# Token mixer of an attention and mixer kernel: the second token product of three batches by seven block products, added into XT by accumulating DMA

## The chip, the cores and the metric

The kernel runs on one core of a Trainium2 chip. The metric is the device time in microseconds (us); lower is better. A core has four engines that compute: TensorE (PE in the profile; its weight loads are PEld), VectorE (DVE), ScalarE (ACT) and GpSimd (POOL). A fifth, SyncE (SP), issues DMA transfers; ScalarE and GpSimd can issue them too. All transfers run on the same 16 DMA engines. SBUF is the on-chip memory with 128 partitions, PSUM the small memory of eight banks that TensorE writes to, and HBM the memory outside.

## What is computed

Four batches of 768 tokens with eight heads of 64 go through an attention with a hash mask. The result, 512 wide, goes through a mixer: a token part, which mixes the 768 tokens of a batch by way of 256 hidden rows, and a channel part by way of 1536 hidden columns.

```python
x  = attn_out.transpose(0, 2, 1, 3).reshape(B, S, H * D)   # 4 x 768 x 512
xt = x.transpose(0, 2, 1)
h  = np.maximum(xt @ w_tok1, 0.0) @ w_tok2                 # the token part
u  = x + h.transpose(0, 2, 1)
h2 = np.maximum(u @ w_ch1, 0.0) @ w_ch2                    # the channel part
return u + h2
```

All of it is float32; the weights come as 64-bit words and are turned into float32 on the chip. The change lies in the token part, at `@ w_tok2` and at `x + h`.

## The kernel before

The program is one sequence of three stages, and within each stage the order on every engine is the order in which the code is written (with small shifts where the builder interleaves independent work). An engine takes its instructions in that order; one that waits holds up all behind it.

**Attention** (`attention`, the first 317 us) leaves its result in XT, an SBUF tile of 128 partitions x 4 channel blocks x 3072 tokens: the transposed x. `bounce` (line 236) writes each pair of channel blocks to HBM, turned by VectorE 32 x 32 at a time, and `fetch` (line 251) reads a batch back with tokens on the partitions. During this stage the class `Conversion` (line 140) turns the weights W1, W2 and WC1 into float32.

**Tokens** (`tokens`, line 598, from 317 to 400 us) is the stage of the change. For each batch b, `mix1(b)` multiplies x by W1 (line 629: two banks of 128 x 512, six products each), and ScalarE writes the Relu to r1 (line 636). `mix2(b)` multiplies r1 by W2: for each of four channel blocks and two halves of the tokens, two products of 128 x 384 add up in a bank (line 648), and VectorE adds the bank into XT in place (line 654). The order is mix1(0), mix1(1), mix2(0), mix1(2), mix2(1), mix1(3), mix2(2), mix2(3). Between these, `job()` takes the next piece of side work from a list: two sums of the first channel weights (`weight_sums`, line 668, 7 us of VectorE together), and then the conversion of the second channel weights in eight steps (`Conversion.one`, line 220). A step is five VectorE operations on 768 columns (lines 179 to 199), a square on ScalarE that is written over the raw words (line 208), and an ending on VectorE (line 209) which sets very small words to zero. `inputs(0, T, 0)` (line 587) makes two of the operands of the next stage from XT, after mix2(1).

**Channels** (`channels`, line 687, from 400 us) computes the channel part for 1024 tokens at a time, three times. It already uses a scheme of seven products of blocks in place of eight (`hidden`, `product`): sums and differences of blocks are prepared on VectorE, and the seven results are put together by additions. While the first 1024 tokens go through `hidden` (six times, 12 us each), a list made by `prepare` (line 966) is worked off, one entry in the middle of each `hidden` and one after it: sums of the second weights WC2 into SW2, and their blocks stored to HBM by SyncE. In the second `hidden`, `residual(0)` (line 1197) has SyncE write XT of these tokens to the output, to which the results of the channel part are later added by accumulating DMAs that GpSimd issues (line 1154). At its end a flag is tested; a slower path for large inputs follows, which these inputs do not take.

Of the kernel before, what the change touches and what calls it, by code (L numbers as in the profile page):

```python
# [36 lines left out]
F32 = mybir.dt.float32  # L37
# [11 lines left out]
def kernel(  # L49
# [13 lines left out]
    nc = tc.nc  # L63
# [76 lines left out]
    class Conversion:  # L140


        def __init__(self, pool, parts, bufs):
            self.pool, self.bufs = pool, bufs
            self.todo = [
                (w, dst, rows, j, n)
                for w, dst, rows, blocks in parts
                for j in range(*blocks, rows)
                for n in range(0, dst.shape[2], NW // rows)
            ]  # L150
            self.fetched, self.begun, self.ready = [], None, None
            for _ in range(bufs - 1 or 1):
                self.fetch()

        def fetch(self):
# [15 lines left out]
        def begin(self):  # L171
            if not self.fetched:
                return
            raw, to, rows = self.fetched.pop(0)
            hi = raw[:, :, 1]
            tmp = self.pool.tile([P, 2, NW], F32, name="tmp", tag="cvt", bufs=self.bufs - 1)
            big = tmp[:, 0].bitcast(U32)

            nc.vector.tensor_scalar(
                big, hi, 3, 0x3FFFFFFF, op0=ALU.logical_shift_left, op1=ALU.bitwise_and,  # L180
            )
            nc.vector.scalar_tensor_tensor(
                big, hi, 0xC0000000, big, op0=ALU.bitwise_and, op1=ALU.bitwise_or,
            )
            self.begun = raw, tmp, to, rows
# [16 lines left out]
        def end(self):  # L202

            if not self.ready:
                return
            size, big, to, rows = self.ready
            self.ready = None
            nc.scalar.activation(size, size, ACT.Square)
            nc.vector.scalar_tensor_tensor(
                to, size.rearrange("p (t n) -> p t n", t=rows), LEAST * LEAST,  # L210
                big.rearrange("p (t n) -> p t n", t=rows), op0=ALU.is_ge, op1=ALU.mult,
            )
# [4 lines left out]
            self.fetch()  # L217
            self.begin()

        def one(self):  # L220

            before, self.ready = self.ready, None
            self.begin()
            self.join()
            self.ready, after = before, self.ready
            self.end()
            self.ready = after
            self.fetch()

    pairs = [(b, hp) for b in range(B) for hp in range(NP)]  # L230

# [1 line left out]
    dram = ctx.enter_context(tc.tile_pool(name="dram", bufs=1, space=bass.MemoryType.DRAM))  # L233
    bounced = [dram.tile([S, DM], F32, name=f"bounced{b}") for b in range(B)]

    def bounce(pool, n):

        b, hp = pairs[n]
        stage = pool.tile([P, S // 32, 2, 32], F32, name="stage", tag="stage", bufs=1)
        for k in range(2):  # L240
            nc.vector.transpose(
                stage[:, :, k], XT[:, hp + k, S * b : S * b + S].rearrange("p (a i) -> p a i", i=32),
            )
        to = bounced[b].rearrange("(a i) (g c) -> g i a c", i=32, g=4)
        for g in range(4):
            nc.sync.dma_start(
                out=to[g, :, :, 32 * hp : 32 * hp + 64],
                in_=stage[32 * g : 32 * g + 32].rearrange("p a k i -> p a (k i)"),
            )
# [16 lines left out]
    def attention(pool, psum, W1, W2, x0):  # L266
# [202 lines left out]
        for n in range(len(pairs)):  # L469
            halves = [Half(n, half) for half in range(2)]  # L470
            if n:
                load_v(n + 1)
            for now in halves:
                now.scores()
                now.add()
                if now.half == 0:
                    now.add_last()
            if before:
                before.sums()
            if n + 1 < len(pairs):  # L480
                hashes(n + 1)
            halves[1].add_last()
            if n == 0:
                load_v(1)
            load_qk(n + 2)
            add_values(n)
            if before:
                before.newton()
            weights.join()
            halves[0].weigh()  # L490
            if n + 1 == len(pairs):
                before.divide()
                before = Quotients(halves)
                before.sums()
                before.newton()
                weights.turnover()
                halves[1].weigh()
                break
            if before:
                before.divide()  # L500
            weights.turnover()
            halves[1].weigh()
            if n and n % 2 == 0:
                bounce(pool, n - 2)
            if n == 2 * NP:
                fetch(0, x0)
            before = Quotients(halves)
# [87 lines left out]
            nc.vector.tensor_tensor(T[1], XT[:, high, b], T[0], op=ALU.subtract)  # L595
            nc.vector.tensor_tensor(T[3], XT[:, high, a], T[1], op=ALU.subtract)

    def tokens(pool, psum, W1, W2, x0, weights, jobs, T):

        x1 = pool.tile([P, NR, DM], F32, name="x1", tag="x1", bufs=1)
        R1 = {}
        turned = not jobs
        if not turned:
            fetch(1, x1)
            jobs = jobs(weights(pool))
            bounce(pool, len(pairs) - 2)

        def job():
            if not turned and jobs:
                jobs.pop(0)()

        def bank(name):
            return psum.tile([P, 512], F32, name=name, tag="mm", bufs=4 if turned else 8)

        def banks():
            return psum.tile([P, 2, 512], F32, name="trp", tag="tr", bufs=2)

        def mix1(b):
            x = (x0, x1)[b % 2]
            if b and turned:
                turn(b, x, banks)
            r1 = pool.tile([P, NJ, DM], F32, name="r1", tag="r1", bufs=2)
            for j in range(NJ):
                ps = bank("t1")
                for r in range(NR):
                    nc.tensor.matmul(  # L629
                        ps, W1[:, r, P * j : P * j + P], x[:, r], start=(r == 0), stop=(r == NR - 1),  # L630
                    )
                to = r1[:, j]
                if not turned:
                    to = to.rearrange("p (c g i) -> p g c i", c=NCB, i=32)
                    ps = ps.rearrange("p (g c i) -> p g c i", c=NCB, i=32)
                nc.scalar.activation(to, ps, ACT.Relu)
                job()
            R1[b] = r1
            if not turned and b + 2 < B:
                fetch(b + 2, x)  # L640

        def mix2(b):
            r1 = R1.pop(b)
            for cb in range(NCB):
                for half in range(2):
                    ps = bank("t2")
                    for j in range(NJ):
                        nc.tensor.matmul(  # L648
                            ps[:, :HALF], r1[:, j, P * cb : P * cb + P],
                            W2[:, j, HALF * half : HALF * half + HALF],  # L650
                            start=(j == 0), stop=(j == NJ - 1),
                        )
                    u = XT[:, cb, S * b + HALF * half : S * b + HALF * half + HALF]
                    nc.vector.tensor_tensor(u, ps[:, :HALF], u, op=ALU.add)
                if cb % 2:
                    job()

        for b in range(B):
            mix1(b)
            if b:  # L660
                mix2(b - 1)
            if b == 2:
                inputs(0, T, 0)
        mix2(B - 1)
        while not turned and jobs:
            job()

# [19 lines left out]
    def channels(pool, psum, SW1, second, TA, judge):  # L687
# [278 lines left out]
        def prepare():  # L966
# [42 lines left out]
            def hidden_parts(name):  # L1009
# [6 lines left out]

            sums = weight_sums(WC2, SW2, slice(0, HC), slice(HC, NHT), low, high)
            return [
                sums, [whole("p1"), second_parts("p7")], *([second_parts(name)] for name in ("p6", "p3", "p5", "p2", "p4")),
                *([hidden_parts(name)] for name in SMALLER),  # L1020
            ]

# [277 lines left out]
    def attention_and_tokens(W1, W2, x0):  # L1300
# [11 lines left out]
        second["tile"] = second_tile  # L1312

        def weights(pool):
            return Conversion(pool, [(w_ch2, WC2, 3, (0, NHT))], bufs=3)

        def jobs(conversion):
            return [
                *weight_sums(
                    WC1, SW1, slice(0, NCB // 2), slice(NCB // 2, NCB),  # L1320
                    slice(0, DCH // 2), slice(DCH // 2, DCH),
                ),
                *[conversion.one] * (NHT * DM // NW + 1),
            ]

        inside(tokens, W1, W2, x0, weights, jobs, [TA[:, 0], None, TA[:, 1], None])

    def careful_attention_and_tokens(W1, W2, x0):
        def weights(pool, psum):
            conversion = Conversion(pool, [(w_tok1, W1, 3, (0, NR)), (w_tok2, W2, 1, (0, NJ))], bufs=3)  # L1330
            while conversion.fetched or conversion.ready:
                conversion.one()

        def turned(pool, psum):
            turn(0, x0, lambda: psum.tile([P, 2, 512], F32, name="trp", tag="tr", bufs=2))
# [2 lines left out]
        inside(weights)  # L1338
        inside(turned)
        TA = big["TA"]  # L1340
        inside(tokens, W1, W2, x0, None, None, [TA[:, 0], None, TA[:, 1], None])

    with_token_weights(attention_and_tokens)
    flags = []
# [47 lines left out]
```

## Time and profile before

| what | us |
| --- | --- |
| three runs | 808.86, 809.01, 808.11 (median 808.86) |
| profiled execution | 808.87, of which the profile shows a span of 807.1 |
| token stage | 316.89 to 399.57 |
| first token products (L629), busy | 41.8, 96 records |
| second token products (L648), busy | 41.8, 128 records |
| additions into XT (L654) | 32 of 0.552 each |
| an accumulating store to HBM, 512 KB (L1154) | 5.7 to 11.6 from issue to landing, median 7.7 |

A float32 product is two records on TensorE. Records of matmuls overlap, so a product's price is the length of a stretch over the number of products in it, not the mean of a record. In the lists of instructions in order of time, a line has start, length, engine, line of the code, operation, output and input; what stands in brackets is the time for which the engine stood idle before it, and what ended that. The chain that ended last follows the work back from the last instruction; what lies on it sets the end.

### The profile page before, as it was taken

What the parts mean: (1) busy time and instruction counts of PE and PEld (TensorE: products, weight loads), DVE (VectorE), ACT (ScalarE), POOL (GpSimd) and SP (SyncE); (2) the same over time, 40 slices, a digit from 0 to 9 for tenths busy, and PEclk for the clock granted to TensorE, in tenths of its full rate; (3) what the DMA queues carried; (4) which work ended last, traced back from release to release, by engine and by line L of the source; (5) the groups of instructions that cost most, each with busy time, mean ns of one, the idle gap of its engine ahead of it and who ended that gap; (6) DMA issues with size and microseconds to landing.
All of it is one profiled execution on the core that took longest, in us unless ns stands there. A gap on an engine that the chain in (4) does not pass through costs nothing.

```text
span 807.1 us, 10537 instructions
## 1 busy us (share of the span) xinstructions
PE 798.4 (99%) x3901; PEld 475.0 (59%) x3901; DVE 662.0 (82%) x869; ACT 427.7 (53%) x675; POOL 42.6 (5%) x69
## 2 busy tenths in 40 slices
PE   9999999999999999999999999999999999999996
PEld 5544444444444444455544448876666886666885
DVE  4789999999998677899475969888669897778985
ACT  5688888888888886121022221237773335775111
POOL 1000000000000000000010110011100012000001
PEclk9999999999999999999999999999999999999999
DMA  4435353537353424561008994499754578730455
GB/s 161 143 137 159 120 160 121 160 120 238 128 162 107 140 65 159 178 232 59 0 9 301 325 339 178 162 284 257 252 142 138 218 206 203 239 107 1 166 178 106
DMA packets 88490, 132.30 MB, mean 164 GB/s; under 512 B 29480, under 2 KB 62704, under 8 KB 86128
## 3 DMA queue, kind: packets, MB, share of 16 engines
q1 hardware_dynamic: 82320, 112.60, 41.5%
q0 software_dynamic: 5552, 18.35, 9.4%
q8 instruction: 33, 0.54, 0.3%
q10 hardware_dynamic: 560, 0.61, 0.2%
q14 instruction: 25, 0.20, 0.1%
HBM read 97.21 MB, written 33.69 MB: 162 GB/s over the span
## 4 chain that ended last, share of the span: by engine, by line
PE 97%; DVE 1%; SPq 1%; issue 0%; DMA 0%; ACT 0%; DVEq 0%; ACTq 0%
PE b L715 50%; PE sc L345 19%; PE acc L397 15%; PE t L629 5%; PE t L648 5%; PE sums L421 2%; PE hp L306 1%; DVE esd L383 1%; SPq L316 1%; PE hw L324 0%; PE idle L459 0%; DMA bits<-g 0%; DVE esd L379 0%; DVE bits L326 0%; DVE esd L386 0%
## 5 line engine op out<-in xcount | busy, mean ns | idle before, releaser
L352 ACT ACTIVATE e<-sc 128x768 f32<-128x768 f32 x192 | 154.2, 811 | 14.9 <-PE sc L345 14.6
L345 PE MATMUL sc<-qk 64*128 64x384 f32 x768 | 157.0, 487 | 0.0
L715 PE MATMUL b<-R,second 128*128 128x256 f32 (+1 forms) x612 | 150.9, 404 | 0.0
L721 ACT COPY c<-b 128x512 f32<-128x512 f32 (+1 forms) x78 | 37.5, 488 | 187.4 <-PE b L715 174.0
L715 PEld LDWEIGHTS b<-R,second 128*128 128x128 f32 x612 | 116.3, 190 | 31.6 <-issue 17.0
L397 PE MATMUL acc<-e,vn 128*64 128x384 f32 x768 | 127.6, 488 | 0.0
L383 DVE TENSOR_TENSOR esd<-esd,e 128x768 f32<-128x768 f32 x96 | 92.0, 958 | 10.0
L397 PEld LDWEIGHTS acc<-e,vn 128*64 128x64 f32 x768 | 53.6, 137 | 73.3 <-issue 72.0
L345 PEld LDWEIGHTS sc<-qk 64*128 64x128 f32 x768 | 68.0, 187 | 47.8 <-issue 45.7
L715 PE MATMUL b<-XT,WC 128*128 128x256 f32 (+1 forms) x264 | 82.5, 457 | 0.0
L715 PEld LDWEIGHTS b<-XT,WC 128*128 128x128 f32 x264 | 50.2, 190 | 29.6 <-issue 25.1
L345 PE MATMUL sc<-bits 64*128 64x384 bf16 x384 | 64.1, 323 | 0.8 <-DMA bits<-g 0.6
L379 DVE SCALAR_TENSOR_TENSOR esd<-e 128x768 f32<-128x768 f32 x32 | 30.3, 948 | 19.5 <-ACT e L352 19.4
L629 PE MATMUL t<-x,W 128*128 128x512 f32 x96 | 41.8, 593 | 0.0
L648 PE MATMUL t<-W,r 128*128 128x384 f32 x128 | 41.8, 486 | 0.0
L442 ACT COPY rec<-rec 32x384 f32<-32x384 f32 x64 | 32.6, 509 | 10.0 <-DVE rec L436 9.5
L345 PEld LDWEIGHTS <-bits 64*128 64x128 bf16 x384 | 20.2, 94 | 26.8 <-DMA bits<-g 1.4
L648 PEld LDWEIGHTS t<-W,r 128*128 128x128 f32 x128 | 24.3, 190 | 17.6 <-issue 1.4
L715 PE MATMUL b<-XT,SW 128*128 128x256 f32 (+1 forms) x120 | 34.6, 422 | 0.0
L715 PE MATMUL b<-TA,WC 128*128 128x512 f32 x72 | 33.8, 592 | 0.0
L715 PE MATMUL b<-TA,SW 128*128 128x512 f32 x72 | 32.9, 592 | 0.0
L756 POOL TENSOR_TENSOR c<-c 128x512 f32<-128x512 f32 x6 | 8.0, 1339 | 456.7 <-ACT c L721 435.2
(177 smaller groups left out, 1093.2 us busy)
## 6 DMA issues: line engine op xcount, KB each, us to landing
second<-left SPq DMA_DIRECT2D x18, 1344.0 KB
raw<-in_moe_w_ch SPq DMA_DIRECT2D x16, 768.0 KB
qk<-in_qk SPq DMA_DIRECT2D x15, 768.0 KB
seen<-in_qk POOLq DMA_DIRECT2D x21, 384.0 KB, 3.8
WC<-hidden_left SPq DMA_DIRECT2D x15, 448.0 KB
vn<-in_v SPq DMA_DIRECT2D x16, 384.0 KB
vt<-in_vT SPq DMA_DIRECT2D x16, 384.0 KB
bounced<-stage SPq DMA_DIRECT2D x32, 192.0 KB
```

Source lines behind the costliest of these rows:

```text
L306: nc.tensor.matmul(ps[32 * j : 32 * j + 32, :HALF], projblk, loaded[n][0][:, j % 2, sl], start=True, stop=True,)
L345: nc.tensor.matmul(sc[:, i, :HALF], t[rows, 1, P * c : P * c + P], t[rows, 0, qs], start=start, stop=not start,)
L352: nc.scalar.activation(e, sc[:, :, :HALF], ACT.Exp, scale=SCALE)
L379: nc.vector.scalar_tensor_tensor(self.d, es[0], NR * EPS, es[1], op0=ALU.add, op1=ALU.add,)
L383: nc.vector.tensor_tensor(self.d, self.d, e, op=ALU.add)
L397: nc.tensor.matmul(acc[D * i : D * i + D], vn[:, i, c], e[:, i], start=(c == 0), stop=(c == NR - 1),)
L421: nc.tensor.matmul(ps[at : at + 32], ones[:, :32], self.halves[h].d[:, i], start=True, stop=True,)
L442: nc.scalar.copy(rec[other : other + 32, h], rec[at : at + 32, h])
L629: nc.tensor.matmul(ps, W1[:, r, P * j : P * j + P], x[:, r], start=(r == 0), stop=(r == NR - 1),)
L648: nc.tensor.matmul(ps[:, :HALF], r1[:, j, P * cb : P * cb + P], W2[:, j, HALF * half : HALF * half + HALF], start=(j == 0), stop=(j == NJ ...
L715: nc.tensor.matmul(ps, left(k), right(k), start=start and k == ks[0], stop=stop and k == ks[-1], skip_group_check=True,)
L721: nc.scalar.copy(c, ps)
```

## The change

For batches 1, 2 and 3, r1 (256 x 512, transposed) and W2 (256 x 768) are each taken as 2 x 2 blocks. Four sums of blocks of r1 (`left_sums`) and four of W2 (`weight_sums`, once) are made by VectorE, and seven products take the place of eight, in two halves m of 128 rows each: seven products of 128 x 384 in four banks, three of them added to what a bank already holds after that has been copied. Batch 0 keeps its eight products a half. In all batches the results no longer go from the bank into XT: ScalarE copies, and for batches 1 to 3 VectorE and GpSimd additions, leave them in one of three places (the later SW2, 1536 columns each, taken in turn), and GpSimd issues a DMA of 768 KB that adds a place into XT.

```diff
-        def mix2(b):
-            r1 = R1.pop(b)
-            for cb in range(NCB):
-                for half in range(2):
-                    ps = bank("t2")
-                    for j in range(NJ):
...
-                    u = XT[:, cb, S * b + HALF * half : S * b + HALF * half + HALF]
-                    nc.vector.tensor_tensor(u, ps[:, :HALF], u, op=ALU.add)
-                if cb % 2:
-                    job()
+        def left_sums(b):
+            r1, new = R1[b]
+            a00, a01, a10, a11 = (r1[:, k, NQ * i : NQ * i + NQ] for i in range(2) for k in range(2))
+            nc.vector.tensor_tensor(new[:, 1], a00, a10, op=ALU.subtract)
+            nc.vector.tensor_tensor(a10, a10, a11, op=ALU.add)
+            nc.vector.tensor_tensor(new[:, 0], a10, a00, op=ALU.subtract)
+            nc.vector.tensor_tensor(new[:, 2], a01, new[:, 0], op=ALU.subtract)
+
+        def mix2(b, m):
...
+            ps = [bank("t2")[:, :HALF] for _ in range(4)]
+            to = places[(2 * b + m + 1) % 3].rearrange("p (i n t) -> p i n t", i=2, n=2)
+            p1, u, p7, p57 = (to[:, i, n] for i in range(2) for n in range(2))
+
+            def store():
+                nc.gpsimd.dma_start(
+                    out=XT[:, m::2, S * b : S * b + S], in_=to.rearrange("p i n t -> p i (n t)"),
+                    accum_op=ALU.add,
+                )
...
+            product(0, a00, b00)
+            nc.scalar.copy(p1, ps[0])
+            product(1, a01, b10)
+            product(2, s1, sums[:, 0])
+            nc.scalar.copy(p57, ps[2])
+            product(3, new[:, 1], b01)
+            nc.scalar.copy(p7, ps[3])
+            product(0, new[:, 0], sums[:, 1], False)
+            nc.scalar.copy(u, ps[0])
+            product(2, new[:, 2], b11, False)
+            product(3, a11, sums[:, 2], False)
+            nc.vector.tensor_tensor(p1, ps[1], p1, op=ALU.add)
+            nc.gpsimd.tensor_tensor(p57, p7, p57, op=ALU.add)
+            nc.vector.tensor_tensor(p57, p57, u, op=ALU.add)
+            nc.vector.tensor_tensor(p7, ps[3], u, op=ALU.add)
+            nc.vector.tensor_tensor(u, ps[2], u, op=ALU.add)
+            store()
 
         for b in range(B):
             mix1(b)
             if b:
-                mix2(b - 1)
-            if b == 2:
-                inputs(0, T, 0)
-        mix2(B - 1)
+                left_sums(b)
+                mix2(b - 1, 0)
+                job()
+                mix2(b - 1, 1)
+            if b == 1:
+                weight_sums()
+        mix2(B - 1, 0)
+        inputs(0, T, 0)
+        mix2(B - 1, 1)
```

The conversion of the second channel weights is changed with it. The square goes to a tile of its own (`apart`, one buffer) and no longer over the raw words; the joined words have one buffer instead of two in this stage; and a step (`slot` in place of `one`) first ends the words of the step before, then fetches, begins and joins the next ones.

```diff
-            tmp = self.pool.tile([P, 2, NW], F32, name="tmp", tag="cvt", bufs=self.bufs - 1)
+            tmp = self.pool.tile([P, 2, NW], F32, name="tmp", tag="cvt", bufs=1)
...
-            nc.scalar.activation(size, size, ACT.Square)
+            hi = size
+            if self.apart:
+                size = self.pool.tile([P, NW], F32, name="size", tag="size", bufs=1)
+            nc.scalar.activation(size, hi, ACT.Square)
...
-        def one(self):
-
-            before, self.ready = self.ready, None
+        def slot(self):
+
+            self.end()
+            self.fetch()
             self.begin()
             self.join()
-            self.ready, after = before, self.ready
-            self.end()
-            self.ready = after
-            self.fetch()
```

Smaller parts: the last `bounce` uses the third place as its staging tile; the two sums of the first channel weights are one job; the list of `prepare` begins with an empty entry, so that its first sums, which write over the places, come after the first `hidden` and all later entries half a `hidden` later; `inputs(0, T, 0)` stands between the two halves of batch 3. In the order in which SyncE issues its transfers, the builder now has the four writes of `residual(0)` and the store of p1's weights inside the token stage: the first write waits for the DMAs into XT of batch 0, the other three and the store stand behind those of batch 1.

## The prediction

> **What bounds the kernel now.** I read the busy shares first, then the chain that ended last, as shares and then in order of time through the token stage. Busy times alone would not do: a matmul's recorded length overlaps the next one's.
>
> ```profile
> PE 798.4 (99%) x3901; PEld 475.0 (59%) x3901; DVE 662.0 (82%) x869; ACT 427.7 (53%) x675; POOL 42.6 (5%) x69
> PE 97%; DVE 1%; SPq 1%; issue 0%; DMA 0%; ACT 0%; DVEq 0%; ACTq 0%
> ```
>
> TensorE is busy for 99% of the span and carries 97% of the chain. The chain in order of time (start, length, what):
>
> ```profile
> 316.89 20.80 PE t L629 x48
> 337.69 10.32 PE t L648 x32
> 348.01 10.30 PE t L629 x24
> 358.31 10.32 PE t L648 x32
> 368.63 10.30 PE t L629 x24
> 378.93 20.64 PE t L648 x64
> 399.57 364.23 PE b L715 x1308
> ```
>
> Each piece begins where the last one ends: no gap from 316.89 to 763.8. So a matmul less is time less, and a wait of TensorE is time lost. One second product of a batch (L648) takes 10.32 us for 16 products of 384 columns (each is two records): 20.64/32 = 0.645 us a product. A first product (L629) takes 10.30 us.
>
> The same stretches in the table of busy times by stage (PE, PEld, DVE, ACT, POOL, then clock, DMA share, GB/s):
>
> ```profile
> 316.89:378.93 62.04, 62.04 (x162) 30.60 (x162) 54.99 (x71) 13.27 (x19) 0.00 (x0) 1.00 0.49 165
> 378.93:399.57 20.64, 20.64 (x66) 12.16 (x65) 11.14 (x18) 0.60 (x1) 0.00 (x0) 1.00 0.00 1
> ```
>
> VectorE is nearly as full as TensorE up to 379 us (54.99 of 62.04), then half empty; ScalarE is mostly free, GpSimd idle, and the DMA engines rest after 379 us.
>
> **What the Trainium skill says.** (1) *SBUF — State Buffer*, "Who interferes with whom": a VectorE instruction with two SBUF inputs and a GpSimd instruction that reads SBUF exclude each other for a whole instruction. The trace agrees. On VectorE and GpSimd:
>
> ```profile
> 419.64 1.28 POOL L756 TENSOR_TENSOR c<-c 128x512 f32<-128x512 f32 x1 [10.75 <-ACT c L721]
> 419.71 1.63 DVE L993 TENSOR_TENSOR seen<-second 128x384 f32<-128x384 f32 x1
> ```
>
> The L993 that meets the GpSimd addition takes 1.63 us; the next one, at 426.36, takes 0.55. (2) *DMA: Bandwidth & Descriptors*, "Queues, rings and completion order": each DMA engine goes round-robin between the queues with work. Accumulating stores (L1154) agree roughly: landing took 5.7 us at 788.44, where nothing else ran, and 11.6 us at 539.34, beside a 1,344 KB load.
>
> **The change part by part, against the span of 807.1 us.**
>
> *Matmuls, on the path.* Batches 1 to 3: 14 products instead of 16, as large as before. 3 x 2 x 0.645 = **-3.87 us**. Batch 0 keeps its 16.
>
> *Copies, on ScalarE, hidden.* 8 for batch 0 and 24 for the others, about 0.49 us each (L721): 16 us in 80 us in which it was busy for 14. Inside a block of seven, a bank's second product waits for the copy of its first: three products (1.94 us) lie between for p1, two (1.29 us) for the others, so a prompt copy costs nothing.
>
> *VectorE, off the path while not late.* It loses 32 additions of 0.55 (L654), and gains 24 additions, 12 left sums of 256 columns (0.42, as L1123) and 4 sums of W2 (0.56, as L994): together about +3 us. The first left and W2 sums end near 353 us and are needed at 359.6.
>
> *Weight words.* The squares go to their own tile (one buffer), so a raw buffer is free a little later or sooner, never on the path: loads that were waited for nowhere keep 5 us or more. The joined words have one buffer instead of two, and a slot ends the previous words before it begins new ones. VectorE now waits for the square, which stands behind a Relu and so behind TensorE; and a square waits for VectorE's previous ending, with copies that TensorE needs queued behind it. The closest case is the last square (378.2 us), which needs the ending at 378.2 worked out below: 0.5 us before it hurts. I take 0, with 1 us as the other bound; a gain is excluded, since TensorE never waited here. In the attention stage the buffer count was already one: nothing changes.
>
> *Last transposes into a place, first two sums as one job, inputs moved.* The transposes still start the stage; the sums run back to back as before. T[0] is ready near 397.8 and is needed 3.44 us into the hidden products: nothing.
>
> *Sums of the second weights half a step later.* They end near 417 instead of 416.4, as TensorE arrives sooner; the steps after them follow within 4 us of before, and SyncE's stores with them. Four operations (2.1 us) move ahead of the first output products on VectorE; the operand built there at 475.26 is used near 485. Hidden.
>
> *Residual writes.* SyncE's queue has three of the four, and the 768 KB store of p1's weights, behind the landing of batch 1's second accumulating store. They leave the crowded 424 to 436 us, where they held nobody up, and meet the next accumulating store, below.
>
> *Accumulating DMAs: the new wait.* Eight of 768 KB, from three places. Block (3,1) (batch 3, second half) fills the place that block (2,0) still sends. ScalarE's p1 copy waits for that landing; behind it queue the other copies of the block, and TensorE's fifth product waits for p1. When does it land?
>
> - VectorE. The step that ends slot 5's words starts when its square is done, 358.35 + 0.49 + 0.91 = 359.75 (Relu L636 and square L208). Then a slot (0.93 + 4.05 = 5.0), left sums 1.7, additions of (1,0) 2.0, slot 5.0, additions of (1,1) 2.0, slot 5.0, last ending 0.93, left sums 1.7, additions of (2,0) 2.0: 385.0. GpSimd's three additions in this stretch, 1.27 x 384/512 = 0.95 each, hold VectorE up by 0 to 2.9: I take 2.9, as VectorE has no gap here. So (1,1) is done at 377.3 and (2,0) at 387.9.
> - Transfer. GpSimd takes 1.21 us to issue (L1154), data begin 0.35 later, landing is noticed 0.4 after the last data (estimated from the store at 788.44, whose data ran from 790 to 793.7: 3.64 us of all engines for 512 KB). For 768 KB inside SBUF there is no row: 2.35 us at the rate of plain traffic (335 GB/s), 5.5 us at the accumulating rate. I take the middle, 4.0.
> - (1,1) lands at 377.3 + 1.21 + 0.35 + 4.0 + 0.4 = 383.3. Then 3 x 512 + 768 KB of SyncE's writes run from 384.3 for 6.5 us (2.36 MB at 0.36 MB/us, rows at 428 to 436), to 390.8. (2,0)'s data begin at 389.5, share 1.4 us with them, and land at 389.5 + 4.0 + 1.4 + 0.4 = 395.3.
> - Need. Block (3,1) begins at 391.4 (399.57 - 3.87 - 4.5, and 0.2 for a bank that VectorE frees late); its fifth product is due 2.58 later, 393.9, so the landing is due at 393.3, 0.63 earlier for copy and handovers. It is late by 2.0, with the 0.2: **+2.2 us**.
>
> Sum: -3.87 + 2.2 = **-1.7 us**, a span of 805.4. The profiled execution took 808.87, the median of the three is 808.86: **807.2 us**. Each us on the transfer counts twice, as batch 1's store also releases SyncE's writes: between 2.35 and 5.5 the sum runs from -3.7 to +1.3.
>
> **The rivals.**
>
> - *No new wait.* Transfers of under 3 us, or VectorE not held up by GpSimd: both put the landing before 393.3 and leave the whole 3.87 us: 805.0 us. For it: plain traffic runs at 335 GB/s. Against: L1154 moved 144.
> - *The wait eats the gain.* At 4.9 us a transfer the landing is near 397.1: 808.9 us. For it: 5.5 is what the only accumulating row scales to.
> - *Slower.* The accumulating DMA inside SBUF is slower than into HBM, as each 3 KB row is read twice and written once there. Place: the same copy. Price: 2 us for each us beyond 4.9; it is 1.6 us slower from 5.7 us on, and at 6.5 gives +3.3: 812.2 us. For it: beside other traffic a store took 11.6 us. A wait beyond 3.4 us might also cost TensorE its clock (*TensorE: Matmul & The Clock Gate*, "What's actually happening"); no gap that long is in this trace.
>
> **How the numbers follow.** Chances: a wait of about 2 us (807.2) 0.40; no wait (805.0) 0.25; gain eaten (808.9) 0.17; slower (812.2) 0.18. 0.2%, or 1.6 us, is about what a measurement of this kernel can tell from no change. Half of the first case lies beyond it: faster 0.46, same 0.36, slower 0.18. Range: 804.7, the full gain and 0.3 for the spread of the runs, to 810.2, a transfer of 5.5 us; about 0.15 lies above.
>
> **What would show it.** Right: 28 records for each of batches 1 to 3, no gap of TensorE before 391, one gap near 394 whose releaser is ScalarE's p1 copy, itself released by the DMA into XT; the issue of (2,0)'s store near 388; landing times of 6 to 8 us. Wrong: a gap at a block's first products (VectorE late with sums or banks), a gap behind a square, or gaps in the hidden products from the shifted weights; no gap at all says that transfers or VectorE are faster than taken.

## The result and the profile after

The changed kernel takes 817.6 us (median of six runs, 815.75 to 819.71), the kernel before 808.9 in the same series (808.11 to 810.19): a ratio of 1.0107, with a 95% interval of 1.0089 to 1.0125. The forecast was 807.2 us with a range from 804.7 to 810.2, so the kernel became slower where a gain was forecast, and its time lies outside the range. The profiled execution took 816.98 us, with a span of 815.1 where before it was 807.1.

On the page of the profile after, the busy shares and the shares of the chain:

```profile
PE 799.5 (98%) x3889; PEld 473.8 (58%) x3889; DVE 667.7 (82%) x877; ACT 441.5 (54%) x707; POOL 60.1 (7%) x83
PE 92%; DVE 3%; issue 2%; POOL 1%; SPq 1%; ACT 0%; DMA 0%; DVEq 0%; POOLq 0%; ACTq 0%
```

Twelve product records fewer, as meant, and yet TensorE shows more busy time, so some records are longer. Its share of the chain falls from 97% to 92%; VectorE goes from 1% to 3%, and GpSimd and "issue" (an engine that waits for nothing that the profile shows) come in. The chain in order of time (start, length, what):

```profile
317.61 20.80 PE t L639 x48
...
359.03 9.04 PE t L690 x28
...
368.08 0.55 DVE second L705
...
381.78 0.99 POOL second L706
...
389.75 1.21 POOL XT L673
390.96 1.03 POOL second L706
391.99 6.96 issue
...
398.96 1.22 POOL XT L673
400.18 1.04 POOL second L706
...
401.24 0.56 DVE second L707
...
402.78 1.21 DVE TA L592
...
405.04 0.56 DVE second L705
...
405.65 24.71 PE b L774 x53
```

The saving is there: a batch of seven products takes 9.04 us instead of 10.32. But from 368.07 to 405.65 no piece of the chain is TensorE's. To 381.78 it is mostly VectorE's work (left out here but for its first line). Then it hangs on GpSimd: the addition of block (2,0) (L706), the store of that block (L673 at 389.75), the addition of block (2,1) behind it, then 6.96 us in which GpSimd seems to wait for nothing, the next store, the next addition, and only then VectorE, which ends with the addition (L705) that the hidden stage waits for. The stretches around the two stops of TensorE, in the table of busy times (PE, PEld, DVE, ACT, POOL, then clock, DMA share, GB/s):

```profile
394.88:399.26 4.38, 0.00 (x1) 0.00 (x1) 0.00 (x0) 0.53 (x2) 0.30 (x1) 1.00 0.54 100
399.26:403.20 3.94, 3.89 (x6) 1.67 (x6) 1.93 (x4) 1.19 (x3) 1.95 (x2) 0.57 0.69 125
403.20:405.65 2.45, 0.00 (x1) 0.00 (x1) 2.45 (x4) 0.00 (x0) 0.03 (x1) 1.00 0.66 120
405.65:412.00 6.35, 6.35 (x11) 2.79 (x12) 3.70 (x5) 0.58 (x1) 2.21 (x2) 0.73 0.68 124
```

TensorE stands still for 4.38 us, does its last three products at a clock of 0.57 (3.89 us where 3 x 0.645 = 1.94 would do), stands still again for 2.45, and starts the hidden stage at 0.73. Against the span of before:

| where | us |
| --- | --- |
| the token stage starts later (317.61 for 316.89; it lies between 316.4 and 317.8 in all these profiles, changed or not) | +0.72 |
| six products fewer | -3.87 |
| stop before the fifth product of block (3,1) | +4.38 |
| slow clock in the three products after it (3.89 us for 1.94) | +1.95 |
| stop before the hidden stage (2.49 in the list of TensorE's instructions) | +2.49 |
| short waits before 394.88 (what is left of the stage) | +0.4 |
| hidden and later products, 366.2 us instead of 364.23: the slow start | +1.96 |
| sum | +8.0 |

Two waits have to be explained, then, and the clock follows them. ScalarE's list of instructions names the cause of the first one:

```profile
398.73 0.48 ACT L695 COPY second<-t 128x384 f32<-128x384 f32 x1 [7.20 <-DMA XT<-second]
```

The copy of p1 stood for 7.20 us until the store of block (2,0) had landed. This is the wait that the prediction named. For the second one, GpSimd's list:

```profile
389.75 1.21 POOL L673 DMA_DIRECT2D XT<-second  x1 [6.99 <-DVE second L709]
...
398.96 1.22 POOL L673 DMA_DIRECT2D XT<-second  x1 [6.97 <-issue]
...
405.62 1.21 POOL L673 DMA_DIRECT2D XT<-second  x1 [4.41 <-DVE second L705]
```

The store at 398.96 has had its data since 393.64 (the end of VectorE's last addition of that block). It comes 0.3 us after the store of 389.75 has landed (8.9 us from issue to landing, at 398.65); the next one, 405.62, again comes 0.3 us after a landing (6.3 us from 398.96). GpSimd seems unable to have two of these transfers in flight. The store at 389.75, by contrast, waited for its data: VectorE was done with them at 389.34. The releaser in brackets of the last line, L705, is an addition of block (3,1), which this store doesn't need; its own data were ready at 402.86.

The addition of block (3,0) stands on GpSimd behind the store of 398.96 and begins at 399.74. VectorE had waited for it for 7.13 us when it went on at 401.24. Behind that stand the rest of that block's additions, then the two operations of `inputs` (L592, L593), which the change has moved between the halves of batch 3, and only then L705. So both stops go back to the landing at 398.65: the first directly, by the place, the second by way of GpSimd's queue. But `inputs` is part of the second stop too: it takes VectorE from 402.78 to 405.04, 2.26 us, with a stop of 2.49. No run puts it behind L705.

### The profile page after: what moved, and what is told of

It is laid out like the page before. It is cut to its first block, busy times and chain, and to the rows that moved or that the text cites. A ratio compares the mean times of both kernels' runs of the same rounds, so it can differ in the third digit from the quotient of the medians.

```text
span 815.1 us, 10615 instructions
## 1 busy us (share of the span) xinstructions
PE 799.5 (98%) x3889; PEld 473.8 (58%) x3889; DVE 667.7 (82%) x877; ACT 441.5 (54%) x707; POOL 60.1 (7%) x83
## 4 chain that ended last, share of the span: by engine, by line
PE 92%; DVE 3%; issue 2%; POOL 1%; SPq 1%; ACT 0%; DMA 0%; DVEq 0%; POOLq 0%; ACTq 0%
PE b L774 49%; PE sc L345 18%; PE acc L397 15%; PE t L639 4%; PE sums L421 2%; PE t L682 1%; PE t L690 1%; PE hp L306 1%; DVE esd L383 1%; PE hw L324 1%; SPq L316 1%; POOL second L706 0%; PE idle L459 0%; POOL XT L673 0%; DVE tmp L179 0%
## 5 line engine op out<-in xcount | busy, mean ns | idle before, releaser
L774 PE MATMUL b<-R,second 128*128 128x256 f32 (+1 forms) x612 | 150.9, 404 | 0.0
L774 PEld LDWEIGHTS b<-R,second 128*128 128x128 f32 x612 | 116.3, 190 | 31.6 <-issue 17.2
L383 DVE TENSOR_TENSOR esd<-esd,e 128x768 f32<-128x768 f32 x96 | 92.0, 958 | 10.0
L774 PE MATMUL b<-XT,WC 128*128 128x256 f32 (+1 forms) x264 | 84.3, 464 | 2.5 <-DVE second L705 2.5
L774 PEld LDWEIGHTS b<-XT,WC 128*128 128x128 f32 x264 | 50.7, 192 | 34.0 <-issue 26.0
L673 POOL DMA_DIRECT2D XT<-second x8 | 9.9, 1237 | 385.3 <-ACT second L686 340.2
L774 PE MATMUL b<-XT,SW 128*128 128x256 f32 (+1 forms) x120 | 34.6, 422 | 0.0
L774 PE MATMUL b<-TA,WC 128*128 128x512 f32 x72 | 33.8, 592 | 0.0
L774 PE MATMUL b<-TA,SW 128*128 128x512 f32 x72 | 32.9, 592 | 0.0
L386 DVE TENSOR_TENSOR esd<-esd,e 128x768 f32<-128x768 f32 x32 | 30.5, 953 | 1.8
L639 PEld LDWEIGHTS t<-x,W 128*128 128x128 f32 x96 | 18.2, 190 | 22.7 <-issue 21.5
```

The costliest lines, as they stand in the source:

```text
L383: nc.vector.tensor_tensor(self.d, self.d, e, op=ALU.add)
L386: nc.vector.tensor_tensor(self.d, self.d, self.es[-1], op=ALU.add)
L639: nc.tensor.matmul(ps, W1[:, r, P * j : P * j + P], x[:, r], start=(r == 0), stop=(r == NR - 1),)
L673: nc.gpsimd.dma_start(out=XT[:, m::2, S * b : S * b + S], in_=to.rearrange("p i n t -> p i (n t)"), accum_op=ALU.add,)
L774: nc.tensor.matmul(ps, left(k), right(k), start=start and k == ks[0], stop=stop and k == ks[-1], skip_group_check=True,)
```

## The experiments

Two theories stood at the start. **A (queue)**: GpSimd can't issue an accumulating store while another is in flight, and the additions queued behind it come late. **B (place)**: the wait of block (3,1) for its place is the only cause, and the second stop and the clock follow from it. All results in one table; the token stage runs from its first product to the first product of the hidden stage in the chain, "rest" from there to the end of the span, both from the one profiled execution, and the ratio is to the kernel before, timed on the same chip.

| kernel | median us | ratio, 95% interval | token stage | rest |
| --- | --- | --- | --- | --- |
| before | 808.9 | | 82.68 | 407.5 |
| changed | 817.6 | 1.0107 (1.0089 to 1.0125) | 88.04 | 409.5 |
| ring_after | 812.82 | 1.0042 (1.0025 to 1.0058) | 85.48 | 409.0 |
| fourth | 816.57 | 1.0086 (1.0073 to 1.0099) | 87.67 | 409.7 |
| fourth_ring | 814.28 | 1.0051 (1.0037 to 1.0065) | 84.48 | 410.6 |
| ring_before | 809.60 | 0.9999 (0.9989 to 1.0008) | 82.67 | 407.6 |
| dve57 | 811.48 | 1.0032 (1.0020 to 1.0044) | 84.05 | 408.0 |
| fourth_dve57 | 805.21 | 0.9954 (0.9940 to 0.9967) | 78.81 | 408.2 |
| fourth_dve57_ring | 805.99 | 0.9957 (0.9943 to 0.9970) | 78.81 | 407.6 |
| no_residual | 814.11 | 1.0063 (1.0047 to 1.0078) | 85.56 | 410.2 |
| eight | 808.87 | 0.9993 (0.9984 to 1.0001) | 82.67 | 407.7 |

### More room for GpSimd's descriptors (ring_after, ring_before)

```diff
-        "TRN2", target_bir_lowering=False, num_devices=1, dynamic_dma_scratch_size=1024
+        "TRN2", target_bir_lowering=False, num_devices=1, dynamic_dma_scratch_size=1600
...
-    projs = const.tile([P, P + 32], F32, name="projs")
...
     def attention(pool, psum, W1, W2, x0):
+        projs = pool.tile([P, P + 32], F32, name="projs", tag="projs", bufs=1)
```

> The changed kernel with a descriptor area for GpSimd's DMAs of 1,600 instead of 1,024 bytes a partition (to make room, the projections are kept in the attention stage's pool). Theory A (queue): GpSimd can't issue an accumulating store while the one before it is in flight, and the additions queued behind it on GpSimd come late; then VectorE's inputs and the last block, and with them the start of the hidden stage at 405.65, hang on GpSimd. Expected under A: store (2,1) is issued near 394 instead of 398.96, the 2.49 us idle time ahead of the hidden stage goes (it starts near 403.4), the clock is back by then, 813 to 814 us; the 4.4 us idle time ahead of the fifth product stays. Theory B (place): the prediction's wait for the landing of block (2,0) is the only cause, and the rest follows from it: store (2,1) is still issued at 398.9, 817.6 us as before this edit.

> The kernel before with 1,600 instead of 1,024 bytes for GpSimd's descriptors (projections moved as in the others): the control. Theory A: its accumulating stores to HBM (L1154) are issued as soon as VectorE has their data, where the page of before shows 660.60 right behind a landing at 660.27; nobody waits for them, so within 0.2% of 808.9. Theories B and C: the same time, issues unchanged.

Measured: 812.82 us, a ratio of 1.0042, just under the band of theory A. GpSimd's list in ring_after:

```profile
388.67 1.20 POOL L673 DMA_DIRECT2D XT<-second  x1 [6.94 <-DVE second L709]
...
392.97 1.20 POOL L673 DMA_DIRECT2D XT<-second  x1 [2.07 <-DVE second L709]
```

The store of (2,1) now goes out 4.30 us after that of (2,0), which lands only at 397.3: two are in flight, and the 6.97 us of "issue" are gone. The second stop is gone as well; the first remains, at 4.06 us. Theory A holds for the stores, and B, which left no room for this, falls. In the kernel before, the same limit was there and cost nothing. Its GpSimd list, and then that of ring_before:

```profile
539.34 1.21 POOL L1154 DMA_DIRECT2D out<-second  x1 [2.42 <-DVE second L1140]
551.27 1.21 POOL L1154 DMA_DIRECT2D out<-second  x1 [10.72 <-DVE XT L784]
```

```profile
537.65 1.20 POOL L1154 DMA_DIRECT2D out<-second  x1
540.86 1.20 POOL L1154 DMA_DIRECT2D out<-second  x1 [2.01 <-DVE XT L781]
```

Before, 11.9 us lie between these two stores, and the first takes 11.6 to land; with more room it is 3.2 us. The time is the same, since nobody waits for them.

### Another place for block (2,0) (fourth, fourth_ring)

```diff
-            to = places[(2 * b + m + 1) % 3].rearrange("p (i n t) -> p i n t", i=2, n=2)
+            to = x0.rearrange("p r c -> p (r c)")[:, : 2 * S]
+            if turned or (b, m) != (2, 0):
+                to = places[(2 * b + m + 1) % 3]
+            to = to.rearrange("p (i n t) -> p i n t", i=2, n=2)
```

> The changed kernel with block (2,0) sent from a part of x0, free since the first products of batch 2, so that block (3,1) fills a place from which nothing is being sent. Theory A (queue): the idle time of 4.38 us ahead of 399.26 and the slow products behind it go, but the hidden stage still starts near 405.6, since GpSimd's stores and the additions behind them stand where they did: one idle time of 7 to 8 us ahead of the hidden stage, at least as much lost to the clock there as now, 817 to 818.5 us. Theory B (place): the idle time, the slow products and the slow start of the hidden stage go together, 807 to 810 us.

Measured: 816.57 us, a little under the band, and the intervals of this ratio and of the changed kernel's overlap. TensorE's list in fourth (the edit adds three lines, so here and in all kernels that have it L777 is L774, L676 is L673, and so on):

```profile
395.27 0.81 PE L693 MATMUL t<-W2sums,r 128*128 128x384 f32 x2
404.53 5.09 PE L777 MATMUL b<-XT,WC 128*128 128x512 f32 x8 [8.45 <-DVE second L708]
```

The first stop is gone; TensorE is done with the stage at 396, and then stands for 8.45 us, since the hidden stage starts about where it did. The wait that the prediction had named could be removed whole without a gain: behind it, the chain by way of GpSimd was nearly as late. That is A's forecast and speaks against B.

> Both edits together: 1,600 bytes a partition for GpSimd's descriptors, and block (2,0) sent from x0. Theory A (queue): no idle time above 1 us from 388 us to the hidden stage, clock at full there, hidden stage from 397 to 398: 806 to 807.5 us, faster than the kernel before. Theory B (place): the same as with x0 alone. Theory C (the accumulating DMAs themselves, by their traffic or by GpSimd's use of the SBUF port, slow the rest): still above 811 us.

This one missed: 814.28 us instead of 806 to 807.5, in the band of theory C. TensorE still stands 5.34 us before the hidden stage, at 402.27. VectorE's list in fourth_ring:

```profile
396.39 0.56 DVE L710 TENSOR_TENSOR second<-second 128x384 f32<-128x384 f32 x1 [2.22 <-POOL second L709]
...
397.92 1.22 DVE L592 TENSOR_TENSOR TA<-XT 128x1024 f32<-128x1024 f32 x1
399.05 2.70 DVE L593 TENSOR_TENSOR TA<-XT 128x1024 f32<-128x1024 f32 x1
401.68 0.54 DVE L708 TENSOR_TENSOR second<-t,second 128x384 f32<-128x384 f32 x1
```

With free places and free issue, the addition on GpSimd (L709 in this kernel) still stands in GpSimd's queue behind the store of the block before, and that store waits for VectorE's last addition of its block; VectorE in turn waits 2.2 us a block for GpSimd's addition (as at 396.39). The two engines take turns instead of working side by side. L593, which meets the next GpSimd addition at 399.19, takes 2.70 us where L592 takes 1.22. And the addition that the hidden stage waits for (L708) stands behind both, so 3.76 us of VectorE's list ahead of it, from 397.92 to 401.68, are those of `inputs`. So theory A was incomplete: a store that blocks is one part of it, an addition placed behind a store is another, and where `inputs` stands is a third.

### The addition of p7 and p57 on VectorE (dve57, fourth_dve57, fourth_dve57_ring)

```diff
-            nc.gpsimd.tensor_tensor(p57, p7, p57, op=ALU.add)
+            nc.vector.tensor_tensor(p57, p7, p57, op=ALU.add)
```

> The changed kernel with one edit: the addition of p7 to p57 (L706) runs on VectorE instead of GpSimd, so nothing that VectorE waits for stands behind an accumulating store on GpSimd. Theory A (queue of GpSimd): the stores are issued as late as before this edit (store (2,1) only after (2,0) has landed, near 398), so the idle time of about 4.4 us ahead of the fifth product of block (3,1) and the slow products behind it stay; but VectorE reaches the last block's additions early, and the hidden stage follows the last product without the 2.49 us idle time: 812 to 814 us, ratio near 1.004, as with the larger descriptor area alone. Theory D (VectorE): six more additions of 0.47 us on VectorE, which paces the stage, make it no better than the changed kernel: 817 us or more.

> L706 on VectorE, and block (2,0) sent from x0; the descriptor area as in the changed kernel, so the stores still go out one at a time. Theory A: neither of the two waits is left on the path: no idle time above 1 us, hidden stage from 396.5 to 397.5, 805.5 to 807.5 us, ratio near 0.997. Theory E (the stores must be out sooner in any case, since something else waits for their landing): the hidden stage starts no earlier than about 400, above 809 us.

> The kernel fourth_dve57 with 1,600 bytes for the descriptors as well. Theory A: the time of fourth_dve57 within 0.15%, as nothing that waits for GpSimd's stores is on the path any more. Theory E: faster than fourth_dve57 by over 2 us.

dve57 took 811.48 us, a little under its band. The stores are as late as in the changed kernel (388.59, then 397.70), but the second stop is gone; TensorE shows one stop of 3.77 us before the fifth product. VectorE, with six more additions, is no worse, and theory D falls: from the start of the stage, it has the data of store (2,0) ready 0.9 us sooner than in the changed kernel. The edit takes away two things at once, the additions behind GpSimd's stores and the hold-up of VectorE's operations that meet an addition on GpSimd (three took about 2.9 us longer ahead of store (2,0) in the changed kernel). No run separates the two; the wait of 7.13 us in the changed kernel is for the queue. `inputs` stays where it was, and VectorE is done with it at 395.7, before the stop of TensorE ends, so it costs nothing here.

fourth_dve57 took 805.21 us, a little under its band and 0.46% less than the kernel before (interval 0.33 to 0.60%), the shortest median of all. Its chain, from the first batch of seven products on:

```profile
357.85 9.03 PE t L693 x28
366.88 10.30 PE t L639 x24
377.18 18.06 PE t L693 x56
395.24 364.23 PE b L777 x1308
```

No piece is anything but TensorE's, each begins where the last one ends, and the hidden products take 364.23 us as before. The stage is 82.68 - 78.81 = 3.87 us shorter, the six products. GpSimd's list shows that the stores still go out one at a time; this one comes 0.3 us after the landing of the store of block (2,0):

```profile
396.74 1.22 POOL L676 DMA_DIRECT2D XT<-second  x1 [7.87 <-DVE second L710]
```

fourth_dve57_ring, where three stores are in flight at once (issued at 388.76, 391.48 and 394.11, the first landing at 397.8), has the same stage of 78.81 us and the same time within the intervals. With nothing behind the stores that anyone needs, their lateness is free. That also speaks against theories C and E: in these two kernels the transfers themselves hold up nobody on the path.

Read as a square of two edits, the token stage is 88.04 (neither), 87.67 (place), 84.05 (addition), 78.81 (both). The two waits lie one behind the other: removing the first alone lets TensorE reach the second sooner.

### The residual writes left out (no_residual)

```diff
-            if t == 1:
-                residual(0)
```

> The changed kernel without the residual writes of the first 1,024 tokens (four DMAs of 512 KB of L1262 are left out, so that part of the output lacks the residual). Theory of contention: the store of block (2,0) is no longer beside other traffic and lands in 6.3 to 6.8 us instead of 8.9; the idle time ahead of the fifth product falls from 4.38 to about 2 us, the clock doesn't fall, and every later store is issued 2.4 us sooner: 812 to 814 us. Rival: the store's own length decides (the landing of 8.9 us is not from the other writes): landing and time as in the changed kernel.

Measured: 814.11 us, just over the band. The store of (2,0), issued at 388.53, has landed by 395.0, so in 6.4 us instead of 8.9, and the first stop is 1.91 us instead of 4.38. The other 2.5 us of the 8.9 were the traffic of SyncE's residual writes. The expected state of the clock was wrong, however. The time after the stop, microsecond by microsecond, in the table of busy times:

```profile
395.00:396.00 1.00, 0.44 (x2) 0.31 (x3) 0.00 (x0) 0.97 (x3) 0.73 (x1) 1.00 0.00 0
396.00:397.00 1.00, 1.00 (x4) 0.56 (x3) 0.00 (x0) 0.76 (x2) 1.00 (x2) 0.93 0.00 0
397.00:398.00 1.00, 1.00 (x3) 0.33 (x1) 0.45 (x1) 0.00 (x0) 0.52 (x1) 0.50 1.10 197
```

The clock fell to 0.50 near 397, when TensorE had been at work again for 1.3 us, after a stop of only 1.91. A second stop of 3.43 us followed, and the clock came back at 407. So here the contention is worth 2.5 us of landing and of stage, but the clock took a part of it back (rest: 410.2).

The changed kernel's own profile shows how to read this. There the clock is 1.00 or 0.50, and it changes within these four stretches (TensorE's busy time, then clock, DMA share, GB/s):

```profile
399.00:400.00 1.00, 0.74 (x2) 0.73 0.00 0
...
402.00:403.00 1.00, 1.00 (x3) 0.56 1.10 197
...
406.00:407.00 1.00, 1.00 (x3) 0.65 0.00 0
...
409.00:410.00 1.00, 1.00 (x2) 0.65 1.05 194
```

The mean over a stretch gives the moment of the change: 399.46, 402.88, 406.30 and 409.70, each 3.4 us after the one before. In the other kernels that stopped, half clock lasted 3.4 us (dve57), 6.8 us (ring_after, fourth, fourth_ring) and 10.2 us (no_residual): once, twice and three times as long. So the changes lie on a grid with steps of 3.4 us. Counted in these steps, each of the seven falls to half clock in these six profiles follows a step in which TensorE stood still for 1.9 us or more: 1.91 us in no_residual, 2.49 us ahead of the second fall in the changed kernel, 2.56 to 3.4 us in the others. Three steps with 1.0 to 1.2 us of standing still brought no fall. A stop thus need not last a whole step to cost the clock, and the stop of 2.49 us in the changed kernel had a slow stretch of its own.

### Eight products with the accumulating stores (eight)

```diff
-            if not b:
+            if True:
                 for n in range(4):
...
-                left_sums(b)
...
-            if b == 1:
-                weight_sums()
```

> fourth_dve57 with eight block products for all four batches, as batch 0 has them (the sums of blocks of r1 and of W2 and the additions of the products are left out, ScalarE copies every result): what is left of the change is the accumulating DMA and the squares kept apart. If the 3.87 us of products are the whole gain of fourth_dve57 and the accumulating DMAs cost the path nothing once nobody waits for them: 808.5 to 809.5 us, ratio 0.999 to 1.001. If the DMAs or the squares themselves help or cost: outside of 0.9975 to 1.0025.

Measured: 808.87 us, 0.9993 (0.9984 to 1.0001), and a stage of 82.67 us. What is left of the change is its way into XT, the squares of the weight words kept apart and the smaller parts, and the stage is as long as before. So together these cost nothing and bring nothing on this path; the gain of fourth_dve57 is that of the products.

### How many stores fit (ring1040, ring1072)

```diff
-        "TRN2", target_bir_lowering=False, num_devices=1, dynamic_dma_scratch_size=1024
+        "TRN2", target_bir_lowering=False, num_devices=1, dynamic_dma_scratch_size=1040
```

> The changed kernel with 1,040 instead of 1,024 bytes a partition for GpSimd's descriptors, nothing else. If a descriptor has 16 bytes, this is 65 a DMA engine; a store shows 272 packets in the trace, 17 an engine,[...] so I estimate 2 x 16 + 1 = 33 descriptors a store. Theory A: two stores need 66, so at 65 they still go out one at a time: store (2,1) issued after the landing of (2,0), near 398, time as the changed kernel, ratio 1.009 to 1.011. Rival (the area is shared out in another way, any more of it helps): issued near 394 and about 4 us faster.

> The same with 1,072 bytes, 67 descriptors an engine by the same estimate. Theory A: two stores fit, so store (2,1) is issued near 393 while (2,0) is in flight, (3,0) waits for (2,0) and is issued near 398.5, which nobody waits for in time; the hidden stage starts near 402, ratio 1.004 to 1.006. Rival (a store takes 17 or 34 and more, or another number): as with 1,040 bytes.

Neither execution came to an end on the chip (a time-out), so there is no number. What a store takes of the area stays open. The size of 16 bytes in the estimate rests on the Trainium skill, *DMA: Bandwidth & Descriptors*, "Terms", which says that a descriptor has 16 bytes and that those of GpSimd's transfers are written to rings in SBUF. The count of 33 is a guess from the 272 packets of a store. The estimate agrees with one store in flight at 1,024 bytes (64 descriptors) and three at 1,600 (100), but no run tests it between these, and none shows the size of a descriptor.

## Why the prediction was wrong

- **Products, -3.87: right.** 9.04 us a batch in the profile, and 3.87 us of stage between the kernel before (or eight) and fourth_dve57.
- **The place of the wait: right.** ScalarE's p1 copy of block (3,1), released by the landing of block (2,0), TensorE stopped before the fifth product.
- **Its size, +2.2: too small.** The stop was 4.38 us. The landing, 396.0 by the prediction when its start of stage is moved by the 0.72, came at 398.65. Of the 2.65 between, 1.1 is the issue (389.75 for 388.6), 0.4 the transfer (6.3 to 6.4 from issue to landing where nothing disturbed it, for 5.96), 1.1 the share with SyncE's writes (2.5 for 1.4, by the 8.9 beside them and by no_residual). The unknown with the widest bounds, the rate of an accumulating transfer inside SBUF, was nearly right.
- **What was not seen: the queue of GpSimd.** The step "GpSimd takes 1.21 us to issue" priced each store alone, as if it could go when its data were there. It goes when the store before it has landed, 6.3 to 8.9 us later, and the next addition of p57 stands behind it, and VectorE behind that. The prediction asked who waits for the landing, but not who stands behind the store on GpSimd. This is the step that failed: it put at nothing a second stop of 2.49 us, and, as fourth shows, this chain is nearly as late as the first one, so that taking the first stop away won almost nothing (a stage of 87.67 us for 88.04). It is not the whole miss: dve57, which has no such stop, still took 811.48 us, outside the range, by the first stop and the slow clock behind it. The trace of before had the queue: the store at 551.27 was issued 0.3 us after the landing of the one before, though its line named VectorE as the releaser.
- **The clock: named, not priced.** It stood in a rival as what a wait beyond 3.4 us might cost. It cost 1.95 + 1.96 us, nearly half of the loss, and the second of these followed a stop of only 2.49 us.
- **The rival "slower" had the right sign and the wrong mechanism.** It rested on a transfer slower than 5.7 us by its own measure; the transfer's data took about 4.3 (6.3 less issue, start and notice as the prediction put them). That its sign came true is luck.
- **Costs put at nothing: one of them wrong.** For the moved `inputs` the prediction asked when its results are needed, but not what stands behind it on VectorE: with VectorE late, its 2.26 us lay between the additions and the hidden stage. The closest case that the prediction named came true once, with 0.2 us: in block (2,0) the p1 copy stood behind a square that waited for VectorE, and the fifth product began at 380.98 instead of 380.77. As far as the runs show, no other stop comes from the squares, the joined sums or the shifted sums of the second weights; the chains of fourth_dve57 and of eight have no gap in the hidden stage. The hold-up of VectorE by GpSimd's additions was taken as 2.9 us; the three operations that met one there took 1.25, 2.12 and 1.65 us, about 2.9 more in all than alone.

## What to carry to other kernels

A store that GpSimd could not yet issue held up all that stood behind it on GpSimd, here for about 7 us. Before putting computation behind a store there, ask how many such stores can be in flight, and read it off two stores in a row, from the landing of the first to the issue of the second. When one wait is removed and nothing is won, look for a second chain that ends within a few us of it, and remove both. A stop of TensorE of 2 us or more had a second price here, in the slow clock after it (1.95 and 1.96 us in the changed kernel), so a change that saves 4 us can't afford one.

## What the runs showed of the hardware

- With 1,024 bytes a partition for descriptors, GpSimd had one accumulating store of 768 KB in flight; with 1,600 bytes, three (fourth_dve57_ring). With 1,040 and 1,072 bytes the program did not end.
- An accumulating store of 768 KB inside SBUF took 6.3 to 6.4 us from issue to landing where nothing disturbed it, and 8.9 beside SyncE's writes. With three at once the landings were 9.0, 10.0 and 11.7 us after the issue.
- The Trainium skill, *TensorE: Matmul & The Clock Gate*, "What's actually happening", has the clock at half after an idle window of about 3.4 us, and at full after a busy one; the window runs freely. The profiles agree with a free-running window: the changes of the clock within a profile lie 3.4 us or a multiple of it apart, wherever the stops begin, so that in fourth the fall came at 400.5, more than 4 us into the stop, and in no_residual after work had begun again. They don't agree that the window has to be idle throughout: 1.91 us (no_residual) and 2.49 us (the changed kernel) of standing still in a step were enough, 1.0 to 1.2 us were not. What lies between is not tested.
